# Squared-ReLU attention with a gated feed-forward on one core: products of zeros in the first batch, padded values copied on chip, the last tile stored in pieces

## The chip, the cores and the metric

The kernel runs on one core of a Trainium2 chip. The metric is the device time of one execution in microseconds (us). An execution consists of instructions on five engines: PE (TensorE) multiplies matrices, ACT (ScalarE) and DVE (VectorE) compute elementwise and empty PE's accumulators, POOL (GpSimd) here mainly issues the loads, and SP (SyncE) issues the DMA transposes and the stores. Transfers run on 16 DMA engines. Each engine and each DMA queue works in its own order; they wait for each other by semaphores.

## What is computed

For each of 8 batches and 12 heads (448 positions, 64 wide) attention weights are squared ReLUs of the scaled scores, without a softmax. The heads, side by side, go through a feed-forward layer whose gate is a ReLU:

```
scores = matmul(q, k^T) / sqrt(64)
attn   = maximum(scores, 0)**2 / 448
x      = heads of matmul(attn, v) side by side     # 3584 x 768
out    = (maximum(x @ w_gate, 0) * (x @ w_val)) @ w_out   # 768 -> 1536 -> 768
```

Inputs and output are float32; the kernel multiplies in bfloat16 and the loads convert. The constant factors are put together into one and applied to the output.

## The kernel before, in words

**Attention.** A slot is one pair of heads of one batch: 48 slots, six to a batch. The 448 positions are cut into three groups of 128 and one of 64. `burst` (L193) issues six matmuls that give the transposed scores of the three full groups of both heads; `scores_last` (L188) gives those of the short group. For the short group the two heads share one tile: keys and values of that group are padded, one head in the left half, the other in the right, zeros elsewhere. `relu2` (L185) is a ReLU on ACT from PSUM to SBUF (L179) and a square on DVE (L183). `av` (L204) multiplies attention by values: six matmuls for the full groups from `v_b`, two for the short group from the padded `vp_b`, and a cast to `xT` on DVE (L213). `mm2` (L64) makes two matmuls of 64 output rows from one of 128.

**Keys and queries transposed.** In batches 0 and 1 PE transposes (`transposes`, L163: eight products with an identity for the keys, eight for the queries, then one DVE copy into `kq_sb`). From batch 2 on `dma_transposes` (L135) copies keys and queries on DVE into `kr` and `qr` (L140) and SP issues eight DMA transposes into `kT` and `qT` (L143). It is called in slot 2 of the batch before, `key_pads` (L145) in slot 4.

**Feed-forward.** A `gv_unit` (L228) makes 128 of the 1536 columns of gate and value for one batch, 24 matmuls, with a ReLU on ACT (L236, tile `g_sb`) and a product on DVE (L241, tile `hT`). An `out_unit` (L253) makes half (384 columns) of one output tile of 128 rows, 24 matmuls, copied on ACT (L262); after the second half two stores of 64 rows go from SP (L265). The units of one batch are dealt out over the slots of the next: `gap` (L287) takes the next ones from a list. The last batch's units stand alone at the end.

**Order.** Every operation is pinned, so each engine works in the order of the code. In batch 0 a slot is: `burst`; ReLU and square of the first group; transposes for the next slot; ReLU and square of the other groups; `scores_last`; then `av` of the slot before. After slot 5 `av` follows for that slot itself. Then five feed-forward units, the transposes of batch 1's first slot and a sixth unit. In later batches `av` is that of the same slot.

**Loads.** All loads are issued by POOL, in the order of L295 to L306: keys and queries of batch 0 for heads 0 and 1, then 2 to 5, the values, keys and queries of heads 6 to 11; three of five chunks of the gate and value weights; batch 1; two chunks; the output weights. The loads of batch b + 1 are issued after slot 0 of batch b (L347). Each load of keys, queries or values is two DMAs, for 64 partitions each: a run of four consecutive positions of a head per partition (256 positions) and a run of three (192). Of the values only three of the four are loaded into `v_b`; the fourth comes by two more DMAs straight into `vp_b` (L107). Eight semaphores are used in turn, so a DMA is issued when the eighth before it has landed.

Of the kernel before, what the change touches and what calls it, by code (L numbers as in the profile page):

```python
# [9 lines left out]
FP32 = mybir.dt.float32  # L10
BF16 = mybir.dt.bfloat16
AF = mybir.ActivationFunctionType
# [4 lines left out]
def kernel(  # L17
# [14 lines left out]
    nc = tc.nc  # L32

    B, H, S, D = q.shape
# [16 lines left out]
    atpool = ctx.enter_context(tc.tile_pool(name="atpool", bufs=3))  # L51
    rpool = ctx.enter_context(tc.tile_pool(name="rpool", bufs=4))
    hpool = ctx.enter_context(tc.tile_pool(name="hpool", bufs=1))
    gpool = ctx.enter_context(tc.tile_pool(name="gpool", bufs=4))
    opool = ctx.enter_context(tc.tile_pool(name="opool", bufs=3))
    psum = ctx.enter_context(tc.tile_pool(name="psum", bufs=1, space=bass.MemoryType.PSUM))

    def pin(ins):
        return tc.keep_in_program_order(ins)
# [16 lines left out]
    ident = const.tile([128, 192], BF16, name="ident")  # L76
# [13 lines left out]
    def dma_in(o, i):  # L90
        pin(nc.gpsimd.dma_start(out=o, in_=i))  # L91

    def load_nat(dst, src, b, h0, h1, ni):
        lo = src[b, h0:h1, 0:256, :].rearrange("h (j i) d -> j h i d", i=4)
        hi = src[b, h0:h1, 256:448, :].rearrange("h (j i) d -> j h i d", i=3)
        dma_in(dst[0:64, h0:h1, 0:ni, :], lo[:, :, 0:ni, :])
        dma_in(dst[64:128, h0:h1, 0:3, :], hi)

    def load_qk(b, h0=0, h1=H):
        load_nat(kn_b[b % NB], k, b, h0, h1, 4)  # L100
        load_nat(qn_b[b % NB], q, b, h0, h1, 4)
# [83 lines left out]
    def relu2(src, dst, n):  # L185
        square_part(dst, relu_part(src, n))
# [14 lines left out]
            todo.append((ps[:, :, :S], attn[:, 2 * i:2 * i + 2, :], 2))  # L201
        return todo

    def av(b, hp, attn, xT):  # L204
        if b < PE_B:
            ps = psum.tile([128, 512], FP32, name="xT_ps", tag="acc", bufs=2)[:, :S]
# [6 lines left out]
        pin(nc.vector.tensor_copy(xT[:, hp, :], ps))  # L213
# [39 lines left out]
    def out_unit(b0, t, hf, hT, state):  # L253
        if hf == 0:
            state[t] = opool.tile([128, d_model], FP32, name="o_sb")
        o_sb = state[t]
        o_ps = psum.tile([128, 512], FP32, name="o_ps", tag="acc", bufs=2)[:, :OH]
        m = slice(hf * OH, (hf + 1) * OH)
        for kf in range(KF):
            mm2(o_ps, hT[:, kf, bass.ts(t, 128)], wo_sb[kf // 6][:, kf % 6, m], kf == 0, kf == KF - 1)  # L260
        flush()
        pin(nc.scalar.activation(out=o_sb[:, m], in_=o_ps, func=AF.Copy, scale=float(out_scale)))  # L262
        if hf == 1:
            for s in range(2):
                pin(nc.sync.dma_start(out=segment_rows(b0, 2 * t + s), in_=o_sb[s * 64:s * 64 + 64, :]))  # L265

    hT_of, xT_of, o_state = {}, {}, {}

    def ffn_units(b):
        b0 = b - b % 2  # L270
        if b == b0:
            hT_of[b0] = hpool.tile([128, KF, 2 * S], BF16, name="hT")
        hT, xT = hT_of[b0], xT_of[b]
        units = [lambda mf=mf: gv_unit(b, mf, xT, hT) for mf in range(KF)]
        for t in (range(0, 3) if b == b0 else range(3, 7)):
            for hf in range(2):
                units.append(lambda t=t, hf=hf: out_unit(b0, t, hf, hT, o_state))
        return units


# [112 lines left out]
```

## Time and profile before

| what | value |
|---|---|
| median of 3 runs | 446.57 us (446.33 to 449.02) |
| profiled execution | 449.76 us, of which the span from first to last instruction is 447.7 us |
| PE busy | 426.9 us, 95% of the span, 4608 matmuls |
| DVE, ACT busy | 215.2 us, 220.2 us |
| POOL busy | 61.5 us |
| DMA from POOL's queue | 53568 packets, 23.60 MB |
| DMA from SP's queue | 38272 packets, 19.28 MB |
| mean granted clock of PE | 0.994 |

The slices of the page show the busy share of each engine in 40 equal parts (11.2 us each) in tenths:

```profile
PE   3879998899999999999999999999999999999995
DVE  4682566535643556444653457455644445422210
ACT  3572565546454654654464565464455456442221
DMA  7999999997443914398153932471042200030014
```

A line of the timeline gives the start in us from the span's beginning, the busy time, the engine, the line of the program, the operation, what it writes and reads, its shape and how many are merged; in brackets stands the time that the engine was idle just before, and what ended it. A matmul's end is modelled and overlaps the next one's, so starts are compared with starts.

### The profile page before, as it was taken

The page shows a single profiled execution, that of the slowest core. Times are in us where ns is not written, and L with a number is a line of the kernel's source. Part 1 is how long each engine was busy: PE and PEld are TensorE (multiplying, and loading weights), DVE is VectorE, ACT ScalarE, POOL GpSimd, SP SyncE. Part 2 cuts the span into 40 slices and gives each one's busy share as a digit, 9 for nine tenths or more (in the row PEclk, how much of TensorE's full clock was granted, in tenths as well). Part 3 has the DMA queues.
Part 4 walks back from the last instruction along what each step waited for, and adds up shares of the span by engine and source line. Part 5 has one row for each costly group of instructions (what it writes and reads, how often), then busy time and mean ns, then how long its engine had stood idle before and what let it go on. Part 6 is the DMA issues. An engine that isn't in the chain of part 4 may idle for free.

```text
span 447.7 us, 10641 instructions
## 1 busy us (share of the span) xinstructions
PE 426.9 (95%) x4608; PEld 251.4 (56%) x4608; DVE 215.2 (48%) x382; ACT 220.2 (49%) x345; POOL 61.5 (14%) x89
## 2 busy tenths in 40 slices
PE   3879998899999999999999999999999999999995
PEld 1337554545566555665566555565556655666663
DVE  4682566535643556444653457455644445422210
ACT  3572565546454654654464565464455456442221
POOL 9624410430003100050001300020000000000000
PEclk9999999989999999999999999999999999999999
DMA  7999999997443914398153932471042200030014
GB/s 83 181 204 191 202 205 178 151 243 99 45 115 77 204 16 98 63 147 110 39 87 91 191 50 63 98 111 24 19 108 72 72 2 0 5 90 15 1 37 107
DMA packets 91887, 43.55 MB, mean 97 GB/s; under 512 B 66753, under 2 KB 88257, under 8 KB 91841
## 3 DMA queue, kind: packets, MB, share of 16 engines
q0 software_dynamic: 53568, 23.60, 42.6%
q1 hardware_dynamic: 38272, 19.28, 20.1%
q8 instruction: 36, 0.59, 0.5%
q14 instruction: 11, 0.08, 0.1%
HBM read 47.19 MB, written 11.01 MB: 130 GB/s over the span
## 4 chain that ended last, share of the span: by engine, by line
PE 79%; DMA 15%; POOL 2%; SPq 1%; DVE 1%; issue 1%; ACT 0%; POOLq 0%; DVEq 0%
PE g_ps L62 22%; PE o_ps L62 22%; PE v_ps L62 21%; PE sc_ps L62 7%; PE xT_ps L62 6%; DMA qn<-in_q_dram 5%; DMA kn<-in_k_dram 4%; DMA wv<-in_moe_w_val_dram 2%; DMA qT<-qr 2%; DMA vn<-in_v_dram 2%; SPq L143 1%; DVE attn L183 1%; POOL qn L91 1%; POOL wg L91 1%; POOL kn L91 1%
## 5 line engine op out<-in xcount | busy, mean ns | idle before, releaser
L179 ACT ACTIVATE r_sb<-sc_ps 128x896 bf16<-128x896 f32 x192 | 149.5, 826 | 43.7 <-PE sc_ps L62 43.7
L183 DVE TENSOR_TENSOR attn<-r_sb 128x896 bf16<-128x896 bf16 x192 | 104.8, 564 | 75.3 <-ACT r_sb L179 75.3
L62 PE MATMUL g_ps<-xT,wg 128*64 128x448 bf16 x1152 | 126.9, 356 | 0.2 <-DVE xT L213 0.2
L62 PE MATMUL v_ps<-xT,wv 128*64 128x448 bf16 x1152 | 125.7, 354 | 0.0
L62 PE MATMUL o_ps<-wo,hT 128*64 128x384 bf16 x1344 | 117.2, 327 | 0.0
L241 DVE TENSOR_TENSOR hT<-v_ps,g_sb 128x448 bf16<-128x448 f32 x96 | 60.0, 625 | 104.7 <-PE v_ps L62 104.7
L236 ACT ACTIVATE g_sb<-g_ps 128x448 bf16<-128x448 f32 x96 | 52.3, 545 | 106.8 <-PE g_ps L62 106.8
L62 PEld LDWEIGHTS <-hT 128*64 128x64 bf16 x1344 | 74.8, 110 | 38.1 <-issue 5.6
L62 PEld LDWEIGHTS <-wg 128*64 128x64 bf16 x1152 | 63.9, 110 | 48.9 <-issue 11.2
L62 PEld LDWEIGHTS <-wv 128*64 128x64 bf16 x1152 | 66.6, 110 | 43.3 <-issue 1.0
L262 ACT ACTIVATE o_sb<-o_ps 128x384 f32<-128x384 f32 x56 | 27.8, 496 | 72.1 <-PE o_ps L62 72.1
L213 DVE CAST xT<-xT_ps 128x448 bf16<-128x448 f32 x48 | 29.9, 624 | 23.6 <-PE xT_ps L62 22.0
L62 PE MATMUL xT_ps<-attn,vn 128*64 128x448 bf16 x288 | 37.3, 362 | 2.6 <-DVE attn L183 1.6
L91 POOL DMA_DIRECT2D vn<-in_v_dram x16 | 12.1, 765 | 191.0 <-PE xT_ps L62 186.0
L62 PE MATMUL sc_ps<-qT,kT 64*128 64x448 bf16 x216 | 26.7, 352 | 2.8 <-DMA qT<-qr 2.8
L62 PEld LDWEIGHTS <-vn 128*64 128x64 bf16 x288 | 17.0, 112 | 14.0 <-issue 3.8
L62 PE MATMUL sc_ps<-kq_sb 64*128 64x448 bf16 (+1 forms) x96 | 16.1, 417 | 2.3 <-DVE kq_sb L174 1.3
L62 PEld LDWEIGHTS <-kT 64*128 64x128 bf16 x216 | 7.6, 94 | 18.3 <-issue 15.0
L62 PE MATMUL xT_ps<-attn,vp 128*64 128x448 bf16 x96 | 17.7, 362 | 0.0
L91 POOL DMA_DIRECT2D kn<-in_k_dram x20 | 14.8, 768 | 13.6 <-PE kq_ps L172 12.7
L91 POOL DMA_DIRECT2D qn<-in_q_dram x20 | 14.7, 760 | 7.4 <-DMA qn<-in_q_dram 3.9
L91 POOL DMA_DIRECT2D vp<-in_v_dram x16 | 10.8, 692 | 17.1 <-PE g_ps L62 5.3
(27 smaller groups left out, 85.8 us busy)
## 6 DMA issues: line engine op xcount, KB each, us to landing
out_dram<-o_sb SPq DMA_DIRECT2D x56, 192.0 KB, 2.7
vn<-in_v_dram POOLq DMA_DIRECT2D x16, 288.0 KB, 7.2
kn<-in_k_dram POOLq DMA_DIRECT2D x7, 384.0 KB, 9.2
qn<-in_q_dram POOLq DMA_DIRECT2D x7, 384.0 KB, 11.2
wo<-in_moe_w_out_dram POOLq DMA_DIRECT2D x2, 1152.0 KB, 17.7
kn<-in_k_dram POOLq DMA_DIRECT2D x7, 288.0 KB, 10.0
qn<-in_q_dram POOLq DMA_DIRECT2D x7, 288.0 KB, 12.4
wg<-in_moe_w_gate_dram POOLq DMA_DIRECT2D x4, 384.0 KB, 9.5
```

The source lines that it names most:

```text
L62: pin(nc.tensor.matmul(o, lhsT=l, rhs=r, start=start, stop=stop, skip_group_check=True))
L91: pin(nc.gpsimd.dma_start(out=o, in_=i))
L143: pin(nc.sync.dma_start_transpose(out=tr[:, :, i * 128:i * 128 + r], in_=grp[0:r, i, :]))
L179: pin(nc.scalar.activation(r, src, AF.Relu))
L183: pin(nc.vector.tensor_tensor(dst, r, r, ALU.mult))
L213: pin(nc.vector.tensor_copy(xT[:, hp, :], ps))
L236: pin(nc.scalar.activation(g_sb, g_ps, AF.Relu))
L241: pin(nc.vector.tensor_tensor(hT[:, mf, col:col + S], v_ps, g_sb, ALU.mult))
L262: pin(nc.scalar.activation(out=o_sb[:, m], in_=o_ps, func=AF.Copy, scale=float(out_scale)))
```

## The change

- Before anything else PE multiplies a tile of zeros, `blank`, made by a DVE memset: nine pairs of 448-column matmuls before the first transposes, two pairs before the first scores, and in each slot of batch 0 six (slot 0) or two pairs before the transposes of the next slot and one pair after them. They write to an accumulator bank that a later `av` starts afresh.
- In batch 0 `av` runs two slots late: slot 0's after the scores of slot 2; after slot 5 those of slots 4 and 5 follow.
- The values are loaded with all four positions of a run into `v_b`; the two DMAs into `vp_b` go, and two DVE copies (`value_pads`) fill it: in slot 2 of batch 0 before its `av`, in slot 0 of batch 1, and for later batches in slot 4 of the batch before.
- The last output tile of the whole kernel is made as one half and two quarters, and each piece is stored as soon as it is copied; of the six stores the last is issued by ACT, the others by SP.
- `g_sb` has three buffers instead of four.

```diff
-    gpool = ctx.enter_context(tc.tile_pool(name="gpool", bufs=4))
+    gpool = ctx.enter_context(tc.tile_pool(name="gpool", bufs=3))
...
+    blank = const.tile([128, S], BF16, name="blank")
+    pin(nc.vector.memset(blank, 0.0))
...
-    v_b = [const.tile([128, H, NI, D], BF16, name=f"vn{i}") for i in range(NB)]
+    v_b = [const.tile([128, H, 4, D], BF16, name=f"vn{i}") for i in range(NB)]
...
     def load_v(b):
+        load_nat(v_b[b % NB], v, b, 0, H)
+
+    def value_pads(b):
+
         n = b % NB
-        load_nat(v_b[n], v, b, 0, H, NI)
         for h2 in range(2):
-            s = v[b, h2:H:2, 0:256, :].rearrange("h (j i) d -> j h i d", i=4)[:, :, 3, :]
-            dma_in(vp_b[n][h2 * 64:(h2 + 1) * 64, :, h2 * 64:(h2 + 1) * 64], s)
+            p = slice(h2 * 64, h2 * 64 + 64)
+            pin(nc.vector.tensor_copy(vp_b[n][p, :, p], v_b[n][0:64, h2:H:2, 3, :]))
...
+    def idle_matmuls(ps, n):
+
+        for _ in range(n):
+            mm2(ps, blank[:, 0:128], blank, True, True)
...
-        if hf == 1:
+        pieces = b0 == B - 2 and t == 6
+        if pieces or c1 == d_model:
+            m = slice(c0 if pieces else 0, c1)
             for s in range(2):
-                pin(nc.sync.dma_start(out=segment_rows(b0, 2 * t + s), in_=o_sb[s * 64:s * 64 + 64, :]))
+                e = nc.scalar if pieces and s and c1 == d_model else nc.sync
+                pin(e.dma_start(out=segment_rows(b0, 2 * t + s)[:, m], in_=o_sb[s * 64:s * 64 + 64, m]))
...
+            cuts = [0, OH, OH + OH // 2, d_model] if b == B - 1 and t == 6 else [0, OH, d_model]
+            for c0, c1 in zip(cuts, cuts[1:]):
+                units.append(lambda t=t, c0=c0, c1=c1: out_unit(b0, t, c0, c1, hT, o_state))
...
+    bank = av_bank()
+    idle_matmuls(bank, 9)
     kq_next = operands(0, 0)
-    prev = None
+    idle_matmuls(bank, 2)
+    waiting = []
...
         if b == 0:
             relu2(*todo[0])
+            idle_matmuls(bank, 6 if hp == 0 else 2)
             if hp < HP - 1:
                 kq_next = operands(b, hp + 1)
+            idle_matmuls(bank, 1)
             relu2(*todo[1])
             relu2(*todo[2])
             scores_last(kq, attn)
-            if prev:
-                av(*prev)
-            prev = this
+            waiting.append(this)
+            if hp == 2:
+                value_pads(0)
+            if hp >= 2:
+                av(*waiting.pop(0), bank)
+                bank = av_bank()
             if hp == HP - 1:
-                av(*prev)
+                av(*waiting.pop(0), bank)
+                av(*waiting.pop(0))
...
+            if n == HP:
+                value_pads(1)
             av(*this)
...
                 if hp == 4:
                     key_pads(b + 1)
+                    value_pads(b + 1)
```

More of the change, by code (lines that the diff above doesn't have):

```diff
@@ L91, in dma_in, with load_nat @@
         pin(nc.gpsimd.dma_start(out=o, in_=i))
-    def load_nat(dst, src, b, h0, h1, ni):
+    def load_nat(dst, src, b, h0, h1):
         lo = src[b, h0:h1, 0:256, :].rearrange("h (j i) d -> j h i d", i=4)
         hi = src[b, h0:h1, 256:448, :].rearrange("h (j i) d -> j h i d", i=3)
-        dma_in(dst[0:64, h0:h1, 0:ni, :], lo[:, :, 0:ni, :])
+        dma_in(dst[0:64, h0:h1, :, :], lo)
         dma_in(dst[64:128, h0:h1, 0:3, :], hi)
     def load_qk(b, h0=0, h1=H):
-        load_nat(kn_b[b % NB], k, b, h0, h1, 4)
-        load_nat(qn_b[b % NB], q, b, h0, h1, 4)
+        load_nat(kn_b[b % NB], k, b, h0, h1)
+        load_nat(qn_b[b % NB], q, b, h0, h1)
     def load_v(b):
+        load_nat(v_b[b % NB], v, b, 0, H)
+    def value_pads(b):
         n = b % NB
-        load_nat(v_b[n], v, b, 0, H, NI)
         for h2 in range(2):
-            s = v[b, h2:H:2, 0:256, :].rearrange("h (j i) d -> j h i d", i=4)[:, :, 3, :]
-            dma_in(vp_b[n][h2 * 64:(h2 + 1) * 64, :, h2 * 64:(h2 + 1) * 64], s)
+            p = slice(h2 * 64, h2 * 64 + 64)
+            pin(nc.vector.tensor_copy(vp_b[n][p, :, p], v_b[n][0:64, h2:H:2, 3, :]))
     CHUNKS = [(0, 256), (256, 256), (512, 512), (1024, 256), (1280, 256)]
@@ L202, in burst, with av_bank, av @@
         return todo
-    def av(b, hp, attn, xT):
+    def av_bank():
+        return psum.tile([128, 512], FP32, name="xT_ps", tag="acc", bufs=2)[:, :S]
+    def idle_matmuls(ps, n):
+        for _ in range(n):
+            mm2(ps, blank[:, 0:128], blank, True, True)
+    def av(b, hp, attn, xT, ps=None):
         if b < PE_B:
-            ps = psum.tile([128, 512], FP32, name="xT_ps", tag="acc", bufs=2)[:, :S]
+            ps = ps if ps is not None else av_bank()
         else:
@@ L251, in segment_rows, with out_unit @@
         return r[0:256, :].rearrange("(j i) m -> i j m", i=4)[i]
-    def out_unit(b0, t, hf, hT, state):
-        if hf == 0:
+    def out_unit(b0, t, c0, c1, hT, state):
+        if c0 == 0:
             state[t] = opool.tile([128, d_model], FP32, name="o_sb")
         o_sb = state[t]
-        o_ps = psum.tile([128, 512], FP32, name="o_ps", tag="acc", bufs=2)[:, :OH]
-        m = slice(hf * OH, (hf + 1) * OH)
+        o_ps = psum.tile([128, 512], FP32, name="o_ps", tag="acc", bufs=2)[:, :c1 - c0]
         for kf in range(KF):
-            mm2(o_ps, hT[:, kf, bass.ts(t, 128)], wo_sb[kf // 6][:, kf % 6, m], kf == 0, kf == KF - 1)
+            mm2(o_ps, hT[:, kf, bass.ts(t, 128)], wo_sb[kf // 6][:, kf % 6, c0:c1], kf == 0, kf == KF - 1)
         flush()
-        pin(nc.scalar.activation(out=o_sb[:, m], in_=o_ps, func=AF.Copy, scale=float(out_scale)))
-        if hf == 1:
+        pin(nc.scalar.activation(out=o_sb[:, c0:c1], in_=o_ps, func=AF.Copy, scale=float(out_scale)))
+        pieces = b0 == B - 2 and t == 6
+        if pieces or c1 == d_model:
+            m = slice(c0 if pieces else 0, c1)
             for s in range(2):
-                pin(nc.sync.dma_start(out=segment_rows(b0, 2 * t + s), in_=o_sb[s * 64:s * 64 + 64, :]))
+                e = nc.scalar if pieces and s and c1 == d_model else nc.sync
+                pin(e.dma_start(out=segment_rows(b0, 2 * t + s)[:, m], in_=o_sb[s * 64:s * 64 + 64, m]))
     hT_of, xT_of, o_state = {}, {}, {}
@@ L275, in ffn_units @@
         for t in (range(0, 3) if b == b0 else range(3, 7)):
-            for hf in range(2):
-                units.append(lambda t=t, hf=hf: out_unit(b0, t, hf, hT, o_state))
+            cuts = [0, OH, OH + OH // 2, d_model] if b == B - 1 and t == 6 else [0, OH, d_model]
+            for c0, c1 in zip(cuts, cuts[1:]):
+                units.append(lambda t=t, c0=c0, c1=c1: out_unit(b0, t, c0, c1, hT, o_state))
         return units
```

## The prediction

> **What bounds the kernel now.** I read the page's slices first (PE at 9 from 55 us on, DMA at 9 over the first 100 us), then the timeline by stage, the waits, and the trace's records of DMA landings and packets. From 100 us to 427 us the windows have PE busy all the time, so what is won before about 90 us, or after the last matmul, reaches the end, and nothing else. The first batch:
>
> ```profile
> 19.70 0.64 PE L172 MATMUL kq_ps<-ident,qn 128*64 128x128 bf16 x8 [0.42 <-DMA qn<-in_q_dram]
> 22.14 1.11 PE L62 MATMUL sc_ps<-kq_sb 64*128 64x448 bf16 x6
> 25.58 0.74 PE L62 MATMUL sc_ps<-kq_sb 64*128 64x448 bf16 x6
> 28.83 0.74 PE L62 MATMUL sc_ps<-kq_sb 64*128 64x448 bf16 x6
> 32.65 1.18 DVE L213 CAST xT<-xT_ps 128x448 bf16<-128x448 f32 x2
> 33.32 1.32 PE L62 MATMUL g_ps<-xT,wg 128*64 128x448 bf16 x12 [0.15 <-DVE xT L213]
> ```
>
> Scores start at 6.92, 11.56, 17.08, 22.14, 25.58 and 28.83. The same six matmuls take 1.30 us until about 22.9 and 0.74 after: half clock, which the clock column does not show there. A slot takes 3.25 us warm; the first three took 15.2, so 5.5 us look lost. But slot 3's queries landed only at 19.57, and PE waited for them. Then the hand-over from batch 1 to batch 2:
>
> ```profile
> 68.85 0.96 DVE L140 COPY kr<-kn 128x3072 bf16<-128x3072 bf16 x1 [0.43 <-DMA kn<-in_k_dram]
> 69.84 7.22 SPq L143 DMA_TRANSPOSE kT<-kr  x4
> 72.39 0.96 DVE L140 COPY qr<-qn 128x3072 bf16<-128x3072 bf16 x1 [2.58 <-DMA qn<-in_q_dram]
> 77.10 6.16 SPq L143 DMA_TRANSPOSE qT<-qr  x4
> 79.41 1.63 POOL L91 DMA_DIRECT2D kn<-in_k_dram  x2 [12.68 <-PE kq_ps L172]
> 90.51 0.74 PE L62 MATMUL sc_ps<-qT,kT 64*128 64x448 bf16 x6 [2.83 <-DMA qT<-qr]
> ```
>
> DVE waits for batch 2's keys and queries, which land one after another behind all earlier loads; SP issues eight DMA transposes; PE waits 2.83 us for the last, landed at 90.38. A PE that is earlier in batch 0 waits longer here. The next view is the windows (us, then busy time of each engine, granted clock, DMA share, GB/s):
>
> ```profile
> 87.50:90.51 3.01, 0.18 (x2) 0.03 (x1) 0.62 (x1) 0.00 (x0) 2.71 (x4) 1.00 1.38 224
> 90.51:94.60 4.09, 4.09 (x26) 1.87 (x28) 1.25 (x2) 2.65 (x4) 1.61 (x3) 0.58 1.23 306
> ```
>
> After that wait the clock is 0.58 for 4.09 us: some 1.7 us of work lost. The end, from the timeline:
>
> ```profile
> 443.11 0.49 ACT L262 ACTIVATE o_sb<-o_ps 128x384 f32<-128x384 f32 x1 [1.41 <-PE o_ps L62]
> 443.62 1.11 SPq L265 DMA_DIRECT2D out_dram<-o_sb  x2
> ```
>
> The two last stores land at 446.25 and 446.82; the span ends 0.9 later.
>
> **The change, part by part.** *Products of zeros.* The memset of blank is 224 words wide: 0.24 us by the 0.38 us of the 384-word ones, so PE can start at about 1.25. A pair of 448-column matmuls costs 0.37 us cold (three pairs of xT_ps from 20.47 to 21.59) and 0.19 warm (27.95 to 28.52). Nine pairs end at 4.65 against the transposes at 4.55, but the queries gate at 5.40: no cost. Six pairs in slot 0 run from 8.2 to 9.4 (warm) or 10.5 (cold); the next queries land at 10.04. So slot 1 starts at 11.15 (0.4 earlier) or 12.6 (1.0 later). Neither end counts: slot 3's queries come later than either allows.
>
> *Loads.* The value load's first half grows by a third: 1.99 us between landings (batch 1's queries, same shape, 38.69 to 40.68) for 1.54 (its values). The two padded loads go: 0.66 us (45.33 to 45.99). Net 0.2 us a batch, so slot 3's queries land at 19.37, batch 2's keys at 68.3 instead of 68.73, its queries at 71.87 instead of 72.27. Between 7 and 15 us the queue moved only 70 to 190 GB/s against 197 later; fewer packets could win up to 2 us more there (bound: the bytes it fell short by), less 0 if the packets are not the reason. I take 0.2, the nearest rows.
>
> *Slots 2 and 3.* Transposes done at 19.65; then DVE in its order: copy 0.57, squares 0.54, 0.54, 0.37 (pitches at 20.38 to 22.40), the two copies of padded values at 0.25 each (the kp copies, L149): 22.25. Batch 0's first value product stands ahead of slot 3's scores on PE, and its padded matmuls wait for those copies. Scores of slot 3: about 22.5, against 22.14. Behind the copies on DVE wait only xT and the next squares, which are later anyway.
>
> *End of batch 0.* Slots 3 to 5 keep 3.25 us if the clock holds (ReLU and PE in turn set it; zeros run in PE's gaps). ACT starts 0.2 later than before. After the last square DVE now has three xT casts instead of two, 0.6 more, and the first gate matmul needs the second last. Together 33.32 becomes 34.1.
>
> *Batch 1.* The five units hide the loads: its queries land at 42.0, wanted at 45.4; w_out at 65.1, wanted at 69. DVE is free for kr at 68.42 + 0.8 = 69.2 (0.35 later); qr at 72.0 (0.4 earlier), and with it the squares and PE. SP's first four transposes took 7.22 us while loads ran until 77.97; four later in the trace (124.08) take 5.21. With loads ending 0.6 earlier I take 6.6. The last transposes also shared the DMA engines with batch 3's loads (issued 79.41 after PE's last transposes) and with two instruction fetches (packets of 1.46 us at 80.0 and 1.27 us at 86.2, with hardly any other traffic beside the first). Bounds for the landing: batch 3's whole chain takes 13.2 us (117.19 to 130.39), giving 83.4, so no wait; upward, 2 us for one more such pause, 92. I take 90.1, nearest to this batch's own row: 0.3 earlier. PE arrives at 87.1, waits about as long, and falls to half clock as before.
>
> *Other batches.* POOL issues two DMAs fewer (0.69 each), DVE has 0.5 us of copies more per batch at half load, wait-free since values land slots earlier. Three g_sb buffers: the product that frees one comes a unit (2.3 us) later, three deep covers it. Nothing.
>
> *Last tile.* Its second half becomes two pieces of 192 columns. PE: 24 pairs; 128-column transposes start every 29 ns, so weight loads do not bind, and 192 columns cost half of 384: nothing, 0.05 at most. ACT's last copy is shorter by up to 0.2. SP now issues five stores from 441.7 on at 0.5 to 0.6: the fifth starts at about 444.0, the last one before at 444.14; ACT's own goes at 443.5. Landing took 2.69 us from issue for 192 KB. For 48 KB the nearest rows are 2.4 (kn, 48 KB, POOL's queue) and, below, 1.13 from issue to first packet plus 0.6 of packets and semaphore: 1.75. I take 2.1: lands at 446.1, a gain of 0.7 (0.3 to 1.1).
>
> By the Trainium skill ("DMA: Bandwidth & Descriptors", Anatomy of one DMA) a DMA costs a fixed 2.0 us plus its bytes at 436 GB/s; an estimate by it is 2.1 for 48 KB and 2.45 for 192 KB, and the sum would be within 0.1 of mine.
>
> **Sum.** Batch 2 starts 0.3 earlier, the end is 0.7 shorter: 1.0 us. The profiled execution took 449.76 (span 447.7), 3.2 above the median of the runs, 446.57. 449.76 becomes 448.8, and the median 445.6.
>
> **Rivals.** *The front gain is carried through.* For it: 5.5 us of excess in three slots. Against it: queries at 19.57 and 72.27 come off a DMA queue that PE does not drive, at 195 GB/s. It would give 446.57 - 5.5 - 0.7 = 440.4.
> The Trainium skill ("TensorE: Matmul & The Clock Gate", Part 1) says that PE starts at half clock and is released by one busy window of some 3.4 us, and it advises warming it up; by that rule alone zeros from 1.25 us on bring the full clock at about 5 to 8 us. The durations of 1.30 and 0.74 agree with two clocks, the gain does not follow from them.
>
> *The hand-over loosens.* The padded loads leave the queue while transposes run, and the 132 more PE instructions ahead of batch 2 move the fetch of 80.0 elsewhere. If the last transpose lands before 87.1, the 2.83 us go and the 1.7 of half clock with them: 446.57 - 0.7 - 4.5 = 441.4; half of it is 443.6. Against: batch 3's loads still collide.
>
> *Slower: the clock falls in slot 2.* PE has next to nothing from 16.0 to 19.4, as in the 3.01 us before 90.51. Then slots 3 and 4 run as cold ones (5.06 for 3.25): 3.6 later on top of 0.8. Above about 0.4 of delay DVE's kr is late rather than the keys, and so are SP and the transposes; above 2.8 PE itself is. kr 4.4 late, with some 1 made up by an emptier queue, is 3.4 at batch 2: 446.57 + 3.4 - 0.7 = 449.3. Against: a later PE also releases batch 3's loads later, and has no idle window left before 90.
>
> *Nothing happens*: the transposes land as before, and the fifth store, behind four others, lands no earlier: 446.4.
>
> **How the numbers follow.** Forecast 0.50 (own range 444.3 to 446.9), front carried 0.08, hand-over looser 0.17, slower clock 0.13, nothing 0.12. The likeliest gives 445.6. From 441.4 to 448.5 leaves out the front rival and the worst half of the slow one and a tail of the loose one, under 0.2. One per cent, about what a measurement here can tell from no change, is 4.5 us. Faster by more: 0.15 (front and the best of the loose cases); slower by more needs over 451: 0.05; within: 0.80.
>
> **What would show it.** Right: slot 3's scores at 22 to 23 in spite of a warm slot 1; three xT casts before the first gate matmul at about 34; kr near 69, qr waiting for its queries near 72; PE waiting for qT near 90; last landing near 446.1 against 443.1 for the last matmul. Wrong: a first gate matmul before 32, keys landed before 67, no wait for qT, or half clock in slots 3 and 4.

## The result and the profile after

| | before | after |
|---|---|---|
| median (22 executions each, same chip) | 447.26 us (446.27 to 452.63) | 451.55 us (447.84 to 453.73) |
| ratio of the means, 95% interval | | 1.0070 [1.0044, 1.0095] |
| executions above 449 us | 8 of 22 | 18 of 22 |
| profiled execution, span | 449.76, 447.7 | 451.80, 449.9 |

The kernel is slower by 0.7%, 4.3 us by the medians. The times of the kernel before fall into two groups, 446.3 to 447.5 us (14 executions) and 449.0 to 452.6 (8). Those of the changed kernel spread from 447.8 to 453.7: none lies in the first group. Ratios leave out executions over 1.5% above the fastest of their kernel. The profiled executions are both long ones and differ by 2.0 us only. Their steps, in us from the start of the span:

| step | before | forecast | after |
|---|---|---|---|
| slot 3's queries landed | 19.57 | 19.37 | 19.50 |
| scores of slot 3 | 22.14 | 22.5 | 23.35 |
| first gate matmul | 33.32 | 34.1 | 35.28 |
| DVE starts kr / qr | 68.85 / 72.39 | 69.2 / 72.0 | 71.17 / 72.91 |
| SP starts the queries' transposes | 77.10 | | 78.73 |
| POOL issues batch 3's first load | 79.41 | | 80.13 |
| last transpose landed | 90.38 | 90.1 | 93.03 |
| batch 2's first scores | 90.51 | 90.2 | 93.17 |
| last matmul to end of span | 4.66 | 3.9 | 4.39 |

The first batch in the timeline of the changed kernel:

```profile
17.39 0.41 PE L177 MATMUL kq_ps<-ident,kn 128*64 128x128 bf16 x8 [2.04 <-DMA kn<-in_k_dram]
19.64 0.64 PE L177 MATMUL kq_ps<-ident,qn 128*64 128x128 bf16 x8 [1.83 <-DMA qn<-in_q_dram]
...
22.26 0.53 DVE L113 COPY vp<-vn 64x384 bf16<-64x384 bf16 x2
22.55 0.87 PE L62 MATMUL xT_ps<-attn,vp 128*64 128x448 bf16 x2 [0.41 <-DVE vp L113]
23.35 1.30 PE L62 MATMUL sc_ps<-kq_sb 64*128 64x448 bf16 x6
...
34.53 0.76 PE L62 MATMUL xT_ps<-attn,vn 128*64 128x448 bf16 x6 [1.22 <-DVE xT L226]
...
35.28 1.33 PE L62 MATMUL g_ps<-xT,wg 128*64 128x448 bf16 x12
```

PE reaches slot 2 early (14.05 instead of 17.08) and waits 2.04 and 1.83 us for slot 3's keys and queries, which land hardly earlier (17.25 and 19.50, for 17.78 and 19.57). The six score matmuls at 23.35 take 1.30 again: half clock. The last value product waits 1.22 for an accumulator bank: there are two such banks, so it needs the cast of the first of the three products that now stand together. The windows (busy time of PE, PEld, DVE, ACT, POOL, then clock, DMA share, GB/s):

```profile
17.39:24.50 7.11, 4.86 (x34) 2.06 (x34) 3.07 (x7) 1.09 (x2) 4.03 (x6) 0.52 1.46 196
...
93.17:97.00 3.83, 3.83 (x24) 1.67 (x26) 1.25 (x2) 2.08 (x3) 0.00 (x0) 0.60 1.23 309
```

In the trace's clock record the clock is full from 4.05 to 17.70, half for 6.83 us (twice 3.41) until 24.53, and half once more for 3.41 us from 92.80, at batch 2's start. The hand-over to batch 2, timeline:

```profile
71.17 0.95 DVE L145 COPY kr<-kn 128x3072 bf16<-128x3072 bf16 x1
72.14 6.54 SPq L148 DMA_TRANSPOSE kT<-kr  x4
72.91 0.96 DVE L145 COPY qr<-qn 128x3072 bf16<-128x3072 bf16 x1 [0.79 <-issue]
78.73 5.45 SPq L148 DMA_TRANSPOSE qT<-qr  x4
80.13 1.49 POOL L93 DMA_DIRECT2D kn<-in_k_dram  x2 [24.74 <-PE kq_ps L177]
...
93.17 1.30 PE L62 MATMUL sc_ps<-qT,kT 64*128 64x448 bf16 x6 [4.77 <-DMA qT<-qr]
```

kr no longer waits for its keys, which have long landed; DVE itself is late. Batch 3's loads follow the queries' transposes by 1.40 us instead of 2.31, and PE waits 4.77 instead of 2.83. PE itself reaches batch 2 only 0.72 later than before (88.40 for 87.68); the other 1.94 of the 2.66 by which batch 2 starts late are the longer wait. The end:

```profile
445.92 0.55 ACTq L281 DMA_DIRECT2D out_dram<-o_sb  x1
```

ACT's store starts at 445.92, but SP's fifth only at 446.63, behind four that it began at 444.15; the last landing comes at 448.77.

### The profile page after: what moved, and what is told of

Its sections match the earlier page's. It is cut to its first block, busy times and chain, and to the rows that moved or that the text cites. A ratio compares the mean times of both kernels' runs of the same rounds, so it can differ in the third digit from the quotient of the medians.

```text
span 449.9 us, 10844 instructions
## 1 busy us (share of the span) xinstructions
PE 430.7 (96%) x4698; PEld 254.3 (57%) x4698; DVE 219.1 (49%) x399; ACT 220.3 (49%) x346; POOL 50.9 (11%) x73
## 4 chain that ended last, share of the span: by engine, by line
PE 89%; DMA 4%; POOL 2%; DVE 2%; ACT 1%; SPq 1%; issue 1%; POOLq 0%; ACTq 0%; DVEq 0%
PE g_ps L62 25%; PE v_ps L62 24%; PE o_ps L62 23%; PE sc_ps L62 8%; PE xT_ps L62 7%; DMA qT<-qr 2%; DMA qn<-in_q_dram 2%; DVE attn L188 1%; PE kq_ps L177 1%; POOL kn L93 1%; ACT r_sb L184 1%; SPq L148 1%; POOL qn L93 1%; POOL vn L93 0%; DVE kq_sb L179 0%
## 5 line engine op out<-in xcount | busy, mean ns | idle before, releaser
L62 PE MATMUL o_ps<-wo,hT 128*64 128x384 bf16 (+1 forms) x1368 | 117.3, 324 | 0.0
L275 ACT ACTIVATE o_sb<-o_ps 128x384 f32<-128x384 f32 (+1 forms) x57 | 27.9, 490 | 71.8 <-PE o_ps L62 71.8
L226 DVE CAST xT<-xT_ps 128x448 bf16<-128x448 f32 x48 | 29.9, 625 | 24.5 <-PE xT_ps L62 22.9
L62 PE MATMUL xT_ps<-attn,vn 128*64 128x448 bf16 x288 | 36.0, 357 | 1.2 <-DVE xT L226 1.2
L62 PEld LDWEIGHTS <-kT 64*128 64x128 bf16 x216 | 7.7, 94 | 20.4 <-issue 17.2
L62 PE MATMUL sc_ps<-kq_sb 64*128 64x448 bf16 (+1 forms) x96 | 14.2, 372 | 1.2 <-DVE kq_sb L179 0.8
L62 PE MATMUL sc_ps<-qT,kp 128*64 128x448 bf16 x72 | 12.8, 352 | 0.0
```

Of the source, the lines that this page charges most:

```text
L62: pin(nc.tensor.matmul(o, lhsT=l, rhs=r, start=start, stop=stop, skip_group_check=True))
L275: pin(nc.scalar.activation(out=o_sb[:, c0:c1], in_=o_ps, func=AF.Copy, scale=float(out_scale)))
```

## The experiments

Two questions: what makes batch 2 start late, and which part of the change brings that about. In the kernels' code `-` and `+` are against the kernel named. Each group of runs shares its runs of the kernel before.

### Parts of the change, one by one

All four against the changed kernel. Without the products of zeros:

```diff
-        for _ in range(n):
+        for _ in range(0):
             mm2(ps, blank[:, 0:128], blank, True, True)
```

> The changed kernel without its products of zeros (the tile of zeros is still made); the result is unaffected. Theory H (the hand-over sets the time: DVE comes late to the copy of batch 2's keys, so the transposes land late): the zeros warm PE early, but slot 3's queries land at 19.5 whatever PE does, and the clock falls again before them, so without zeros slot 3 starts within 1 us of 23.35 and the first gate matmul within 1 us of 35.28; ratio to the kernel before within 0.003 of the changed kernel's 1.007. Theory C (the clock: zeros bring two more changes of clock and these are the loss): without them 2 to 3 us come back, ratio 1.000 to 1.003.

Measured: 451.42 us median, ratio to before 1.0065 [1.0034, 1.0096]. Full clock only from 26.3 on, first gate matmul 35.25, against 35.28 with zeros.

With batch 0's last value product in a scores bank:

```diff
                 av(*waiting.pop(0), bank)
-                av(*waiting.pop(0))
+                av(*waiting.pop(0), sc_tile()[:, 0, :S])
```

> The changed kernel with one edit: the last of the three value products that now stand at the end of batch 0 writes to a bank of the scores' pool, so that it needn't wait for a cast to free an accumulator bank. Theory H: the wait of 1.22 us before it goes, the first gate matmul comes at about 34.1 instead of 35.28, DVE reaches the copy of the keys 1.2 earlier, at about 70.0, and batch 2 starts about 1 us earlier, at 92; ratio about 1.004 to 1.005. Theory D (DMA traffic alone sets the landing of the transposes): the copy is earlier, the landing is not; ratio 1.007.

Measured: 452.36, 1.0094 [1.0062, 1.0125]. First gate matmul 34.17, kr 70.17, both 1.0 to 1.1 earlier; batch 2 starts at 92.33, 0.84 earlier, yet the time is no shorter. So the trace moved as one theory said and the time as the other. In the profiled execution the 0.68 that are left at the last matmul are lost at the end, which takes 5.03 instead of 4.39 because one of SP's short stores takes 1.2 us to issue.

The same, with the copies of padded values ahead of work that DVE would wait for:

```diff
             relu2(*todo[1])
+            if n == HP:
+                value_pads(1)
             late.append(todo[2])
...
-            if n == HP:
-                value_pads(1)
             av(*this)
```

and likewise `value_pads(0)`, right after the first square of slot 2.

> As the run before, and the copies of padded values stand earlier on DVE: in slot 2 of batch 0 after the first square, in batch 1 in the first slot before its first feed-forward unit. Theory H: batch 0 ends another 0.5 to 1 us earlier (PE's wait of 0.41 and 1.19 for the copies goes), and batch 1's first slot loses no 0.86 us; the copy of the keys comes at 68.5 to 69.2, near its 68.85 of before, and batch 2 starts at 89.5 to 91; ratio 0.998 to 1.002. Theory D: batch 2 still at 92 to 93, ratio 1.005 to 1.007.

Measured: 452.67 median, 1.0067 [1.0026, 1.0108]; 11 of 12 executions lie between 450.6 and 453.5, and the profiled one is the twelfth, 445.97. Because that one is so short, the ratio leaves out half of the executions; by the medians (447.58 for the kernel before) it is 1.011. In the profiled one the first gate matmul comes at 30.99, and PE did not wait at batch 2 at all (first scores 88.73). In this trace the front is repaired; the other eleven were not profiled, and their time is not better than the changed kernel's.

With the last tile stored as before:

```diff
-        pieces = b0 == B - 2 and t == 6
+        pieces = False
...
-            cuts = [0, OH, OH + OH // 2, d_model] if b == B - 1 and t == 6 else [0, OH, d_model]
+            cuts = [0, OH, d_model]
```

> The changed kernel with the last tile stored as before (two halves, two stores). All theories: from the last matmul to the end of the span 4.6 us as before instead of 4.4; ratio 1.007 to 1.009. If the pieces cost time through the five stores on SP's queue instead, the ratio falls below 1.006.

Measured: 452.25, 1.0077 [1.0044, 1.011]; last matmul to end 4.65 against 4.39, so the pieces gain about 0.27.

No single part explained the loss, and the two outcomes of one kernel, 446 and 452, suggested a race: batch 3's key and query loads and batch 2's last transposes are both under way at 79 to 93 us.

### Holding batch 3's loads

POOL copies a column of batch 2's first attention tile, into a tile `gate` made for it, before it issues them, so they come at 88 to 92 us, after the transposes:

```diff
         if hp == 0 and 1 <= b < B - 1:
+            if b == 2:
+                pin(nc.gpsimd.tensor_copy(gate, attn[:, 0, 0:1]))
             load_qk(b + 1)
```

In the kernel before, in the changed one, and in the changed one with the bank and the earlier copies:

> The kernel before with one addition: the loads of batch 3's keys and queries stand behind a one-column copy on POOL of batch 2's first attention tile, so that they cannot be issued at 79 us, while batch 2's transposes are under way. Theory X (those loads reach the DMA engines ahead of the last transposes, and the transposes wait behind them): without them the last transpose lands at 84 to 87, PE has no wait at the start of batch 2 and no window of half clock, batch 2 starts at 87.5 to 88; ratio 0.990 to 0.994. Theory F (pauses of the DMA engines at instruction fetches, or SP's own issue, set the landing): it lands at 88 to 90 as before, ratio 0.997 to 1.000.

> The changed kernel with the same addition. Theory X: PE reaches batch 2 at about 88.4 and starts it there, 4.8 us earlier than at 93.17, so that what the change costs PE itself in batches 0 and 1 is all that is left: 0.5 to 1 us over the held kernel before, ratio 0.991 to 0.996. Theory H (only the late copy of the keys matters): the copy is still at 71, the transposes land at 91 to 92, ratio 1.003 to 1.006.

> The changed kernel with the last value product in another bank, the copies of padded values earlier, and the same hold on the loads. Theory X: batch 2 starts at 87 to 88 and the end is 0.3 shorter than before; ratio 0.988 to 0.993, not slower than the held kernel before. If the clock still falls to half in batch 1, because PE is early there and waits for the copies of keys and queries, 1 to 2 us are lost again: 0.992 to 0.996.

| medians | loads not held | loads held |
|---|---|---|
| before | 447.13 | 446.42, 0.9976 [0.9957, 0.9995] |
| changed | 451.55 | 445.92, 0.9959 [0.9938, 0.9979] |
| with bank and earlier copies | 452.67 | 444.90, 0.9936 [0.9911, 0.9961] |

The ratios are to the kernel before in the same group (447.13); the two lower figures without the hold come from the groups above (kernel before 447.26 and 447.58). The changed kernel with the hold, timeline:

```profile
72.17 5.68 SPq L149 DMA_TRANSPOSE kT<-kr  x4
77.90 5.26 SPq L149 DMA_TRANSPOSE qT<-qr  x4
88.35 0.74 PE L62 MATMUL sc_ps<-qT,kT 64*128 64x448 bf16 x6
90.39 0.19 POOL L379 COPY gate<-attn 128x1 bf16<-128x1 bf16 x1 [35.67 <-DVE attn L189]
90.88 1.49 POOL L94 DMA_DIRECT2D kn<-in_k_dram  x2 [0.30 <-issue]
```

Its front is as late as the changed kernel's (first gate matmul 35.31, kr 71.19), yet the last transpose lands at 84.42, 6.5 us after the first of the four was issued, not 14.3; no wait at 88.35, no half clock. No held execution of these three kernels (32) is above 447.5. So the whole loss of the medians, and the 1 to 4 us that the kernel before loses in its longer executions, is this collision. For the kernel before the hold gains less than the 0.990 to 0.994 expected, and by the ratio alone the rival (0.997 to 1.000) would fit; the trace decides: the last transpose landed at 85.02, PE did not wait, and batch 2 started at 89.05, after a window of half clock at 75.0. The Trainium skill ("DMA: Bandwidth & Descriptors", Queues, rings and completion order) says that each DMA engine takes packets in turn from the queues that have work for it. The changed kernel's trace agrees in part: from 87 to 90 us it has 710 packets of POOL's queue and 701 of SP's, nearly one for one, and SP's queue moves 0.17 MB in these 3 us, against 0.53 MB in the 4 us from 80 to 84 with the loads held. But from 83 to 87 us it has 1198 packets of POOL's queue and 349 of SP's, so turns are not shown to be the whole of it.

### Zeros in the kernel before, and later transposes alone

Only the products of zeros, added to the kernel before (the tile of zeros and the helper are left out here):

```diff
+    idle_matmuls(9)
     kq_next = operands(0, 0)
+    idle_matmuls(2)
...
             relu2(*todo[0])
+            idle_matmuls(6 if hp == 0 else 2)
             if hp < HP - 1:
                 kq_next = operands(b, hp + 1)
+            idle_matmuls(1)
```

> The kernel before with the products of zeros alone, in the same places. Theory L (batch 0 is set by the landing of the queries of heads 6 to 11): slot 3 starts at 21.5 to 23 in spite of the full clock from about 5 us on, the first gate matmul comes at 32.5 to 33.5, and the ratio is 0.998 to 1.002. Theory C (the clock sets batch 0): the first gate matmul comes at 28 to 30; the time may still not change.

Measured: 446.85, 1.0007 [0.9973, 1.004]; 3 of 12 executions are above 449. The profiled execution (446.08) is the shortest. Its slot 3 starts at 20.31 and its first gate matmul at 31.30, earlier than the one theory said and later than the other. The hand-over:

```profile
69.00 0.96 DVE L142 COPY kr<-kn 128x3072 bf16<-128x3072 bf16 x1 [2.59 <-DMA kn<-in_k_dram]
...
77.22 5.25 SPq L145 DMA_TRANSPOSE qT<-qr  x4
80.58 1.63 POOL L93 DMA_DIRECT2D kn<-in_k_dram  x2 [13.78 <-PE kq_ps L174]
...
88.78 0.74 PE L62 MATMUL sc_ps<-qT,kT 64*128 64x448 bf16 x6
```

and its windows around 75 us:

```profile
71.00:74.78 3.78, 0.58 (x6) 0.25 (x5) 2.22 (x4) 0.49 (x1) 0.00 (x0) 1.00 1.66 172
74.78:78.20 3.42, 3.38 (x18) 1.08 (x17) 2.42 (x5) 1.53 (x2) 0.00 (x0) 0.50 1.42 124
```

This early front meets the keys' landing: DVE waits 2.59 and 2.60 for keys and queries, PE has 0.58 us of work from 71 to 74.8, and the clock falls to half. PE's last transposes, which free the buffers of batch 3's loads, are late for that; the loads come 3.36 us after the queries' transposes, and the last transpose lands at 88.47, before PE asks for it.

Then the reverse: only the transposes late, by copying the keys three times in DVE's wait for the queries:

```diff
-            pin(nc.vector.tensor_copy(o, nat.rearrange("p h i d -> p i h d")))
+            for _ in range(3 if b == 2 and grp is kr else 1):
+                pin(nc.vector.tensor_copy(o, nat.rearrange("p h i d -> p i h d")))
```

> The kernel before, with the keys' copy kr of batch 2 made three times over, so that it ends at about 71.8 us instead of 69.8, inside the time in which DVE waits for the queries anyway (qr at 72.4 stays). Only SP's transposes are late: kT starts at 71.8, qT at 79.0 to 79.6 instead of 77.1; PE, DVE's squares and batch 3's loads (79.4) stay where they are. Collision theory: the loads now come within 0.5 us of the last transposes' start and get onto the DMA engines ahead of them; last transpose lands at 92 to 94 instead of 90.4, PE waits 5 to 6 us, half clock after it; time 450 to 453 (ratio 1.006 to 1.012) in nearly every execution, though nothing of batch 0 is late. Rival, that the change's loss is its late first batch (first gate matmul 2 us later) carried along on PE: nothing of that is in here, so 447.1 (ratio 0.998 to 1.002).

Measured: 450.17 median (447.26 to 452.98), 1.0051 [1.0017, 1.0085]. Nothing of batch 0 is late (first gate matmul 30.86), and yet 8 of 11 executions are above 449. The profiled one, 449.18, was a mild one: SP started only 1.3 us later and caught up, POOL's loads came 3.03 us after the queries' transposes, and PE waited 1.90. The forecast for the median held, at its lower end; those for the ratio (1.006 or more) and for the trace did not, so no trace shows what made the longer executions long.

### Which part makes batch 0 late, once the collision is gone

With the hold, the bank and the earlier copies, the queries' copy and transposes were also moved one slot behind the keys', so that DVE does not stand 2.6 us for batch 2's queries (`dma_transposes` does one of the two parts at a call):

```diff
-                if hp == 2:
-                    dma_transposes(b + 1)
+                if hp in (2, 3):
+                    dma_transposes(b + 1, hp - 2)
```

> The changed kernel with batch 3's key and query loads held, the last value product of batch 0 in a scores bank, the padded copies earlier, and the queries' copy and transposes one slot after the keys' (so that DVE does not stand 2.6 us for batch 2's queries at 69.5 to 72.1). Collision theory: DVE's squares run on, PE has no gap near 75, batch 2 starts at about 86 instead of 87.3, last transposes land by 86: 443.4 to 444.4 (ratio 0.990 to 0.993). Rival: the queries' transposes, now after their own slot, land later and PE waits for them at 86 to 88: 444.9 or more.

> The same without the products of zeros. The price of the zeros with the collision out of the way. Theory that the DMA queue sets batch 0's slots: within 0.5 us of the kernel with zeros. Rival, that the zeros did gain and the collision hid it: 1.5 to 2.5 us slower than that.

> The kernel before with batch 3's loads held and the queries' copy and transposes one slot later, nothing of the change. DVE's stand of 2.6 us goes: 445.0 to 445.8 (ratio 0.995 to 0.997) against 446.4 with the hold alone. If the change's own parts are worth nothing, the kernel with all of them (0.990 to 0.993) is no faster than this one; if they are worth 1 us or more once the collision is gone, it is.

Measured: with zeros 444.40, 0.9912 [0.9879, 0.9945]; without 442.48, 0.9872 [0.9838, 0.9906]; the kernel before with hold and later queries only 443.24, 0.9885 [0.9854, 0.9917]. The last did 2 us better than expected, and the expectation that the zeros cost nothing was wrong: 1.9 us. Slots 2 and 3 with zeros, timeline:

```profile
18.27 0.42 PE L178 MATMUL kq_ps<-ident,kn 128*64 128x128 bf16 x8 [2.73 <-DMA kn<-in_k_dram]
19.99 0.64 PE L178 MATMUL kq_ps<-ident,qn 128*64 128x128 bf16 x8 [1.30 <-DMA qn<-in_q_dram]
...
22.80 1.30 PE L62 MATMUL sc_ps<-kq_sb 64*128 64x448 bf16 x6
...
34.49 1.44 PE L62 MATMUL g_ps<-xT,wg 128*64 128x448 bf16 x12 [0.15 <-DVE xT L227]
```

and with twelve pairs in slots 1 and 2 instead of two:

```diff
-            idle_matmuls(bank, 6 if hp == 0 else 2)
+            idle_matmuls(bank, 12 if hp in (1, 2) else 6 if hp == 0 else 2)
```

> The kernel with all the repairs and zeros (444.4), with 12 pairs of zeros in slots 1 and 2 instead of 2. If the clock falls in slot 3 because PE idles in slots 1 and 2, it now stays full there or falls for one window of 3.4 us less: first gate matmul 32 to 33.5 instead of 34.5, 442.3 to 443.8 (ratio 0.988 to 0.991). Rival, that the gaps are not what decides the clock, or that the wait for the queries at 18.3 to 20 is enough to lose it: half clock at 18.5 to 25 as before, 444.4 or more.

```profile
19.63 0.41 PE L178 MATMUL kq_ps<-ident,qn 128*64 128x128 bf16 x8 [0.45 <-DMA qn<-in_q_dram]
...
21.11 0.74 PE L62 MATMUL sc_ps<-kq_sb 64*128 64x448 bf16 x6
...
32.10 1.44 PE L62 MATMUL g_ps<-xT,wg 128*64 128x448 bf16 x12 [0.16 <-DVE xT L227]
```

Measured: 443.01, 0.9901 [0.9882, 0.992]; full clock from 4.67 to the end. So the zeros of the change wake PE and then leave it idle at 15.5 to 18.3 us, and the clock is half from 18.55 to 25.38, just when the data arrive; with enough zeros to hold the clock the 1.9 us shrink to 0.5, and nothing is won over no zeros at all. The Trainium skill ("TensorE: Matmul & The Clock Gate", Part 1) says that a free-running window of about 3.4 us decides in both directions, up after a busy one and down after an idle one; the stretches of half clock between full ones agree: 3.41 or 6.83 us in every record here that has one. Warming PE up gained nothing in these runs, where the landing of slot 3's queries sets the pace.

The other part, the value products two slots later, in the kernel before without the rest, and the change with values one slot later as before:

```diff
-    prev = None
+    waiting = []
...
-            if prev:
-                av(*prev)
-            prev = this
+            waiting.append(this)
+            if hp >= 2:
+                av(*waiting.pop(0))
             if hp == HP - 1:
-                av(*prev)
+                av(*waiting.pop(0))
+                av(*waiting.pop(0))
```

> The kernel before with only the value products of batch 0 moved two slots later (no zeros, values and padded values loaded as before, last tile as before). Theory that the delay costs the clock: without the value product between slot 1 and slot 2 PE is idle too much from 13 to 17 us, the full clock comes at 22 to 26 us instead of 16.3 to 22.9, and the first gate matmul at 33.5 to 35.5 instead of 30.9 to 33.3; kr late, so the collision strikes: 449 to 452 (ratio 1.004 to 1.010). Rival, that the delay is innocent and the zeros or the padded copies on DVE are what is late: first gate matmul 31 to 33.3, 447.2 (0.998 to 1.002).

> The changed kernel with the value products of batch 0 one slot later, as in the kernel before; zeros, padded copies and pieces stay. Delay theory: the clock stays full through slots 2 and 3, first gate matmul at 31 to 32.5 instead of 35.3, kr at 69 to 70, the collision strikes less often: 446.5 to 449 (ratio 0.998 to 1.004). Rival, zeros or padded copies make batch 0 late: first gate matmul 34 or later, 450 to 452.

Measured: that part alone 451.33, 1.0074 [1.0045, 1.0104], 8 of 9 above 449: as much as the whole loss, though this kernel was not run with the hold. Its first gate matmul was at 33.43, with full clock from 23.34 and the same 1.22 us wait for a bank before its last value product. That is hardly later than in the profiled execution of before (33.32), which is itself a long one. In the profiles of all kernels without zeros the full clock came at 23.3 to 26.3 with values two slots later (three profiles); with values one slot later it came by 17.2 in five and at 22.9 and 23.1 in two, the profiled execution of before being one of these. The value product that the part moves away was PE's work between slots 1 and 2, at 14.50 to 16.22 in the held kernel before. In the five it starts at 14.3 to 14.7, in the two at 15.44 and 14.99: where it starts late, the clock rises late, as where it is missing. Ten profiles suggest this; no run set it.

```diff
-            if hp == 2:
+            if hp == 1:
                 value_pads(0)
-            if hp >= 2:
+            if hp >= 1:
                 av(*waiting.pop(0), bank)
                 bank = av_bank()
             if hp == HP - 1:
                 av(*waiting.pop(0), bank)
-                av(*waiting.pop(0))
```

The change with values one slot later (this second edit) has a first gate matmul at 31.89 and no half clock there, as expected, and still 7 of 12 executions at 451.4 to 453.1, the other 5 at 446.1 to 447.4 (median 451.51, where 446.5 to 449 was expected; ratio, without the two longest, 1.004 [1.0004, 1.0076]). The longest is the profiled one, timeline (453.06):

```profile
77.96 6.24 SPq L148 DMA_TRANSPOSE qT<-qr  x4
78.91 1.49 POOL L93 DMA_DIRECT2D kn<-in_k_dram  x2 [24.41 <-PE kq_ps L177]
...
93.31 1.31 PE L62 MATMUL sc_ps<-qT,kT 64*128 64x448 bf16 x6 [6.14 <-DMA qT<-qr]
```

So a late front is not needed for the collision, and no single part is its cause: the later value products bring it about alone, and the change without them still has it. What it goes with is the gap from SP's first transpose of the queries to POOL's first load of batch 3. Over all profiled executions without a hold:

| kernel | gap, us | first scores of batch 2 after the queries' transposes start | PE's wait |
|---|---|---|---|
| change, values one slot later | 0.95 | 15.35 | 6.14 |
| change, last tile as before | 1.18 | 14.84 | 5.40 |
| change, scores bank | 1.24 | 14.44 | 4.93 |
| change | 1.40 | 14.44 | 4.77 |
| change, no zeros | 2.26 | 14.92 | 4.39 |
| before | 2.31 | 13.41 | 2.83 |
| before, values two slots later | 2.45 | 13.81 | 3.09 |
| before, late front (below) | 2.48 | 13.39 | 2.64 |
| before, keys copied thrice | 3.03 | 13.20 | 1.90 |
| before, zeros | 3.36 | 11.56 | none |
| change, bank and earlier copies | 3.79 | 11.99 | none |

The order is not strict: the row without zeros waits longer than its gap would place it. In the last two rows PE arrived after the last transpose, which landed 11.25 and 10.26 us after the first was issued, still some 3 us more than with the loads held: there the longer gap went with a weaker collision, not with none. The last three rows, and no other, have the window of half clock near 75 us; two of them ran at 446, all above them at 448.9 to 453.1.

### A late front alone

Twelve pairs of products that nobody reads, between batch 0's last value product and the first gate matmul of the kernel before (the tile of zeros is left out here); then the same with the hold:

```diff
             if hp == HP - 1:
                 av(*prev)
+                ps = psum.tile([128, 512], FP32, name="xT_ps", tag="acc", bufs=2)[:, :S]
+                for _ in range(12):
+                    mm2(ps, blank[:, 0:128], blank, True, True)
```

> The kernel before with twelve pairs of products of zeros (2.3 us at full clock) between the last value product of batch 0 and the first gate matmul; nothing else. Theory that a late front brings the loads into the transposes: first gate matmul at 33 to 35.6, PE no longer waits on DVE near 75 us and shows no half clock there, batch 3's loads come within 2.5 us of the last transposes' start, PE waits 3 us or more for the last transpose; 449.5 to 452 (ratio 1.005 to 1.010), more than three quarters of the executions above 449. Rival, that lateness is only carried: hidden behind the keys' landing (447.2), or at most one for one in the executions that had no reserve (448 to 449), with few above 449.5.

> The same with batch 3's key and query loads held. The late front without the collision: between 446 and 447.5 (ratio 0.997 to 1.001) if the front's lateness is hidden behind the wait for batch 2's keys and queries, so that 3 us or more of the loss in the kernel without the hold is the collision. Rival, that the front's lateness itself costs: 448.5 or more.

Measured (first gate matmul 33.15, with the hold 33.72): 450.14, 1.0053 [1.0026, 1.008], 8 of 12 above 449 (more than three quarters were expected; of the kernel before 4 of 21); with the hold 445.45, half a microsecond below the forecast, 0.995 [0.9926, 0.9974]. The same lateness costs 2.6 us by the medians with the collision and nothing without it. Its hand-over:

```profile
76.63 6.82 SPq L145 DMA_TRANSPOSE qT<-qr  x4
79.11 1.63 POOL L91 DMA_DIRECT2D kn<-in_k_dram  x2 [13.12 <-PE kq_ps L174]
...
90.02 0.94 PE L62 MATMUL sc_ps<-qT,kT 64*128 64x448 bf16 x6 [2.64 <-DMA qT<-qr]
```

The transposes start when they did (76.63); but from 71 to 74.8 PE now has 2.75 us of work where it had 0.58 in the execution with zeros, keeps the full clock, and releases the loads at 79.11 instead of 80.58.

### The version that the runs point to

No zeros, values one slot later as before, hold, later queries; kept of the change are the copies on DVE, the pieces and the three `g_sb` buffers:

> No zeros, values one slot later as before, batch 3's key and query loads held, the queries' copy and transposes one slot after the keys'; kept of the change are the padded copies on DVE (batch 1's earlier in its slot) and the last tile in pieces. First gate matmul near 31, batch 2 starts by 85.3, end 0.3 shorter than with the hold and the later queries alone (443.2): 442.3 to 443.2 (ratio 0.986 to 0.989). Rival, that the padded copies cost DVE time in front: 443.5 or more.

Measured: 442.41, 0.9896 [0.9878, 0.9914]: 1% faster than the kernel before, nearly all from the hold and the later queries, which alone gave 443.24. The expected first gate matmul near 31 did not come: it was at 33.23, with full clock only from 23.1.

## Why the prediction was wrong, point by point

- **The step that failed** is the landing of the last transposes: "I take 90.1, nearest to this batch's own row: 0.3 earlier". It came at 93.03, though PE asked for it at 88.40. The text named batch 3's loads and then priced them as unchanged, from the one row at hand. But that row depends on a gap of 2.31 us between two queues, and the change moves both: SP's side by 1.63, POOL's by 0.72. In the profiles a gap of 1.40 costs PE 4.77, one of 2.31 2.83, those above 3.3 nothing; with the loads held the changed kernel's last transpose lands at 84.42, in time. The bound "upward, 92" was too low too.
- **The front.** Slot 3 came at 23.35 for a forecast of 22.5. DVE began the padded copies at 22.26, where the sum had them done, and PE then ran slot 3 cold, a pair of zeros of 0.38 among it. At the end 0.6 for a third cast was asked; the product that waited 1.22 for a bank was not seen, and cost 0.74 of pitch. Sum: 1.96 instead of 0.8.
- **The slower clock in slot 2**, a rival with 0.13, is what happened (half from 17.7 to 24.5). Its price in front (4.4 with the base case) was too high, and its way to the end was wrong: it was to pass one for one through kr; instead the front moved executions into the collision.
- **The zeros** were costed at nothing because the queries gate. That holds for the slots' starts; it overlooks that a PE that is early and then waits loses its clock. With the collision gone they cost 1.9.
- **Batch 1's padded copies**, "wait-free": their first pair cost 0.86 (slot 1 of batch 1 at 57.06, 2.83 later, against 1.96 at the first gate matmul), since DVE reached them only behind a product that waits for PE.
- **The loads** were to be 0.4 earlier; batch 2's keys and queries landed 0.56 later (69.29 and 72.83).
- **The last tile** gained 0.27, not 0.7: the fifth store started 2.63 later than forecast, 0.18 more than PE's own delay of 2.45, and from the last landing to the end of the span it took 1.14 instead of 0.90. Its landing, 2.14 after its issue, was as forecast (2.1). In two of the eleven profiles with pieces the end took 5.03 and 5.37, longer than without (4.61 to 4.67), since SP took 1.2 and 1.7 us to issue one store.
- **The median.** 449.76 was taken as the median execution plus 3.2, with the same steps. It was an execution of the longer group. No short execution of the kernel before was profiled; in the two short ones of other kernels without a hold (446) PE does not wait at batch 2. If that holds for the kernel before too, the range's low end and the rival that loosens the hand-over subtracted a wait that most executions did not have.

Right: the late queries of slot 3 whatever PE does (19.50 for 19.37), no gain from a warm PE, SP's first four transposes (6.54 for 6.6), and that the hand-over decides.

Not settled: why the same kernel falls on one side or the other in one execution. The traces go with the phase of the clock's window, since all that escaped without a hold show the half clock near 75 us, but no run set that phase. Nor were the padded copies or the pieces tried alone in the kernel before.

## What to carry to other kernels

Transfers of two DMA queues that start within a few microseconds of each other can be a race, as here: look for what releases each of them, and price a change by the gap between them, not by the stage's last duration. When times fall into two groups, first find out to which group the profiled execution belongs. If a transfer has time (here batch 3's loads, issued at 80 and wanted at 117), release it after the one that has none.

## What the hardware showed that was not expected

A slower PE went with a shorter time: of the profiled executions without a hold, those in which the clock fell to half at 75 us ended at 446 (449.2 where the transposes were late on purpose), those that kept it at 448.9 to 453.1. That the slow window is the reason is not shown, since no run set it. Four DMA transposes landed 6.5 to 8 us after the first was issued when the loads were held, and 13 to 15 us after it beside loads that were issued one to three microseconds after them; being issued first did not protect them.
